# Last stage of an FFT-and-GLU backward kernel: complex product on VectorE, half spectra copied on chip, buffers reused, evacuations sorted by type

## The chip, the cores and the metric

The kernel runs on one core of a Trainium2 chip. The metric is the time of one execution on the device in microseconds (us). Five engines work side by side, each through its own queue in order: TensorE (PE, matmuls; PEld its weight loads), VectorE (DVE), ScalarE (ACT), GpSimd (POOL) and SyncE (SP, which here only issues DMAs).

## The reference

The function takes x = A_q of shape [1, 2048, 512] and returns one output and nine gradients. All tensors are bf16.

```python
xn = layernorm(x)                                   # per token, over 512 columns
k_shift = sum over t of k_pad[:, t:t+S, :] * shift_k[:, ks-1-t]   # four taps along time
kv = k_shift * v
y  = irfft(rfft(kv, 4096) * rfft(ssm_k, 4096))[:2048] + kv * ssm_D  # long convolution, per column
s  = xn * y
g  = silu( (sigmoid(xn @ w_gate) * (xn @ w_up)) @ w_down )         # GLU, width 1376
out = x + s * g
# returned: out, and the gradients for q, k, v, shift_k, ssm_k, ssm_D, w_gate, w_up, w_down
```

The gradient of the convolution is again a product of spectra, this time with a conjugate: from the gradient of y one gets the gradient of kv (with the spectrum of ssm_k) and that of ssm_k (with the spectrum of kv).

## The kernel before

**Tiling.** Time has 2048 steps; partition p holds steps 16p to 16p+15, so that an activation is a tile of 128 x (16, 512). The 512 columns are worked in four groups of 128 (`cg` = 0 to 3). The FFT of length 4096 is made of matmuls: `step1`/`step1T` multiply by 16 cosine and sine blocks, `flip`/`flipT` turn the data (by TensorE transposes in the first stage, by VectorE 32 x 32 transposes in the last), `step3`/`step3T` multiply by a small block-diagonal matrix. The way back is `inv3` and then `inv1`.

**Stages.** The first stage runs the forward long convolution (`strK`, `strV`, `strX`) beside the GLU's first half for nine of the sixteen token tiles (`f_gen`). It writes both spectra of every sixteenth part to DRAM (`KK_d`, two tiles of 128 x 1024 for each of 16 parts). The middle stage (`stepB`) runs the rest of the GLU forward and all of its backward, token tile by token tile. The last stage runs three streams: `dW()` makes the three weight gradients (35 blocks of 16 matmuls with 512 or 352 columns each, on operands that are loaded transposed from DRAM by SP), `frontC()` makes the forward transform of the gradient of y, and `backC()` multiplies it with the stored spectra, transforms it back and makes the gradients of k, v, shift_k, ssm_k and ssm_D.

**The part that is changed most, `backC`.** For every group there are four parts (`qq`), numbered n = 4 cg + qq. `step3T` leaves a spectrum in PSUM; it is copied out as `Xc` (one copy of 128 x 1024), and a second time with its two halves swapped as `Xw` (two pieces of 64 x 1024, ScalarE only). Real parts lie in partitions 0 to 63, imaginary parts in 64 to 127. For each of the two stored spectra t, two VectorE products are made, `Xc` by KK and `Xw` by KK. They are not summed on VectorE: `inv3` gets both, with one constant matrix for each, and sums them in PSUM:

```python
inv3([(PP[:, 0], RC1), (KK[:, 0], RS2)], qq - 1, B1)      # L1340
inv3([(PP[:, 1], RC1), (KK[:, 1], RS2)], qq - 1, B2, True)  # L1342
```

`inv3` makes eight matmuls of 128 columns for each of its parts, every one with weights of its own. After the four parts come `inv1` (from B1, the gradient `dkv`), the products `dks = dkv * v` and `dkv * ksh`, two small DMAs that shift the halo of `dks` by one partition, sixteen pairs of matmuls for the gradient of ssm_k (`dKT`, in a view that lies on B1's buffer), a diagonal sum on TensorE (`ps_diag`, reads `kh`), and seven VectorE instructions of 128 x 2048 for the four taps (`dk`, `term`). v is loaded and the gradients of v and k (`o3C`, `o2C`) are written for two groups at a time, 1 MB each, in rows of 512 B.

**Order of the work.** The program does not issue instructions as they are written. `Rec` records every instruction with what it reads and writes, and `order()` then plays them through a table of durations, as a list scheduler: each engine takes the recorded instruction with the lowest number among those that are ready, at most 700 numbers ahead. All engines' queues are written in that order. `run_streams` sets in which proportion the streams are recorded; `backC` is recorded to end when `dW` is at 58%. A copy out of PSUM recorded by `evac` may go to ScalarE or VectorE: ScalarE takes it unless it is late by more than 0.4 us (1.6 us where VectorE has other work soon). PSUM has, in the last stage, two slots of two banks for `step1T`, `step3T`, `inv3`, `inv1` and `dKT` together, two single banks for `dW`, and two for small work.

**Memory.** `Arena` gives out SBUF by first fit. Buffers of the last stage lie on buffers of the middle stage that were just freed.

**Layer norm.** `f_ln2` makes a small VectorE instruction for -mean * rstd (`nmr_all`) and then normalises a token tile of 128 x 512 by one ScalarE activation with that as its bias (L705, L706).

Of the kernel before, what the change touches and what calls it, by code (L numbers as in the profile page):

```python
# [20 lines left out]
D = 512  # L21
# [135 lines left out]
class Op:  # L157
    __slots__ = ("n", "alts", "deps", "succ", "wait", "ready", "dma", "tiles", "done", "fin", "eng", "soft")
# [12 lines left out]
class Rec:  # L171
# [65 lines left out]
    def evac(self, dst, src, n):  # L237
        self.add([("scalar", "copy", (dst, src), {}), ("vector", "tensor_copy", (dst, src), {})])
# [109 lines left out]
    def order(self):  # L348
# [55 lines left out]
        while ndone < len(ops):  # L404
            best = None
            for e in self.ENGS:
# [7 lines left out]
                if either and e in ("scalar", "vector"):  # L414
                    o = min(either, key=lambda o: (max(o.ready, free[e]), o.n))
                    s = (max(o.ready, free[e]), o.n, e, 1)
                    late = free["scalar"] - s[0]
# [124 lines left out]
def gen_fft_consts(nc, ar, negpi, Cf, TB):  # L542
# [65 lines left out]
    nc.vector.tensor_copy(an[:, 3], pr[:, 1])  # L608
# [16 lines left out]
def kernel_impl(ctx, tc, A_q, A_k, A_v, A_shift_k, A_ssm_k, A_ssm_D, B_x, B_w_gate, B_w_up, B_w_down,  # L625
# [32 lines left out]
    BD, RS1, RS2, RC1, BDq = (TB[:, q] for q in range(5))  # L658
# [3 lines left out]
    nmr_all = Ring(ar, [NJ], f32).ap  # L662
# [40 lines left out]
    def f_ln2(i):  # L703
        xj, st = T[i]["xq"], T[i]["st"]
        nc.vector.scalar_tensor_tensor(nmr_all[:, i:i + 1], st[:, 6:7], -1.0, rstd_all[:, i:i + 1], ALU.mult, ALU.mult)  # L705
        nc.scalar.activation(xnA[:, i, :], xj, ACT.Identity, bias=nmr_all[:, i:i + 1], scale=rstd_all[:, i:i + 1])  # L706
# [582 lines left out]
    def ld_KK(n):  # L1289
        if n < 16:  # L1290
            KK = KK_r.next()
            nc.sync.dma_start(KK, KK_d[n // 4, n % 4].rearrange("t p x -> p t x"))
            stC["KK", n] = KK

# [9 lines left out]
    def ld_bwd(cg):  # L1304
        c0, c1 = cg * GW, (cg + 1) * GW
        if cg % 2 == 0:
            stC["vg"] = vg_r.next()
            nc.sync.dma_start(stC["vg"], vC[:, :, c0:c0 + 256])
# [7 lines left out]
    def backC():  # L1316
        for cg in range(NG):
# [3 lines left out]
            for qq in range(5):  # L1321
                if qq < 4:
                    n = cg * 4 + qq
                    while ("Qf", cg) not in stC:
                        yield 0
                    Xc, Xw = Xc_r.next(), Xw_r.next()
# [3 lines left out]
                    KK = stC.pop(("KK", n))  # L1330
                    PP = P_r.next()
                    for t in range(2):
                        nc.vector.tensor_tensor(PP[:, t], Xc, KK[:, t], ALU.mult)
                        nc.vector.tensor_tensor(KK[:, t], Xw, KK[:, t], ALU.mult)
                    ys[qq] = (PP, KK)
                if qq == 2:
                    ld_bwd(cg)
                if qq > 0:
                    PP, KK = ys.pop(qq - 1)
                    inv3([(PP[:, 0], RC1), (KK[:, 0], RS2)], qq - 1, B1)  # L1340
                    yield 2048
                    inv3([(PP[:, 1], RC1), (KK[:, 1], RS2)], qq - 1, B2, True)  # L1342
                    ld_KK(cg * 4 + qq + 2)
                    yield 2048
# [3 lines left out]
            vg = stC["vg"][:, :, (cg % 2) * GW:(cg % 2 + 1) * GW]  # L1348
# [6 lines left out]
            dKT = ar.view(B1_r.blks[0][0], [128, NJ], bf16)  # L1355
# [10 lines left out]
            if cg % 2 == 1:  # L1366
                nc.sync.dma_start(o3C[:, :, c0 - GW:c1], y2A[:, :, c0 - GW:c1])
# [11 lines left out]
            if cg % 2 == 0:  # L1379
                stC["dk"] = dk_r.next()  # L1380
            dk = stC["dk"][:, :, (cg % 2) * GW:(cg % 2 + 1) * GW]
            for lag in range(4):
# [4 lines left out]
                else:  # L1387
                    term = term_r.next()
# [4 lines left out]
            if cg % 2 == 1:  # L1393
                nc.sync.dma_start(o2C[:, :, c0 - GW:c1], stC["dk"])
# [31 lines left out]
    KK_r = Ring(ar, [2, 1024], n=3)  # L1426
    Qg_r = Ring(ar, [4096])
    Ci_r = Ring(ar, [2, 16, 128], at=dg_r.blks[0][0])
# [4 lines left out]
    Xc_r, Xw_r, P_r = Ring(ar, [1024], n=2), Ring(ar, [1024], n=2), Ring(ar, [2, 1024], n=2)  # L1433
    vg_r = Ring(ar, [NJ, 2 * GW])
    ksh_r = Ring(ar, [NJ, GW])
    kh_r = Ring(ar, [NJ + 3, GW])
    term_r = Ring(ar, [NJ, GW])
    dk_r = Ring(ar, [NJ, 2 * GW])
# [9 lines left out]
    for n in range(3):  # L1448
        ld_KK(n)
    nc.sync.dma_start(Ci.rearrange("p c j n -> p (c j n)"), Ci_d[:])  # L1450
# [70 lines left out]
```

## Time and profile before

| what | value |
|---|---|
| median of the three runs | 527.73 us (527.04 to 529.77) |
| the profiled execution | 528.14 us, of which the span on the engines 526.4 us |
| PE busy over the span | 491.4 us (93%) |
| DVE busy | 403.5 us (77%) |
| ACT busy | 342.4 us (65%) |
| POOL busy | 124.1 us (24%) |
| granted TensorE clock | 0.997 |

By stage, in us (busy time of each engine within the stretch):

| stretch | length | PE | DVE | ACT | POOL | what runs |
|---|---|---|---|---|---|---|
| 0 to 27 | 27 | 14.7 | 21.2 | 20.7 | 10.5 | loads, constants |
| 27 to 150 | 123 | 113.6 | 98.1 | 120.7 | 54.0 | first stage |
| 150 to 170 | 20 | 18.4 | 15.2 | 11.8 | 5.0 | transposed weights arrive |
| 170 to 336 | 166 | 162.7 | 147.3 | 68.9 | 51.9 | middle stage |
| 336 to 363 | 27 | 26.8 | 11.4 | 8.0 | 1.5 | its end, `dW`, `frontC` of group 0 |
| 363 to 504 | 141 | 137.0 | 101.5 | 107.9 | 1.2 | `backC` with `dW` and `frontC` |
| 504 to 526.4 | 22.4 | 18.1 | 8.7 | 4.3 | 0.0 | rest of `dW`, last taps, last writes |

How to read it: an engine's busy time counts its instructions, not its waiting. Matmuls are pipelined, so PE's busy time is a little more than what its work would need at best. A row of a group list gives the engine, the operation, out<-in by the program's names, the shapes, the count, then busy time in us and the mean in ns of one, then the idle time just before and what ended it. Here nearly every tile lies in one SBUF buffer called slab, and every instruction is issued by one helper line, so groups are told apart by shape and by time.

### The profile page before, as it was taken

The page shows a single profiled execution, that of the slowest core. Times are in us where ns is not written, and L with a number is a line of the kernel's source. Part 1 is how long each engine was busy: PE and PEld are TensorE (multiplying, and loading weights), DVE is VectorE, ACT ScalarE, POOL GpSimd, SP SyncE. Part 2 cuts the span into 40 slices and gives each one's busy share as a digit, 9 for nine tenths or more (in the row PEclk, how much of TensorE's full clock was granted, in tenths as well). Part 3 has the DMA queues.
Part 4 walks back from the last instruction along what each step waited for, and adds up shares of the span by engine and source line. Part 5 has one row for each costly group of instructions (what it writes and reads, how often), then busy time and mean ns, then how long its engine had stood idle before and what let it go on. Part 6 is the DMA issues. An engine that isn't in the chain of part 4 may idle for free.

```text
span 526.4 us, 13494 instructions
## 1 busy us (share of the span) xinstructions
PE 491.4 (93%) x5373; PEld 349.4 (66%) x5429; DVE 403.5 (77%) x777; ACT 342.4 (65%) x455; POOL 124.1 (24%) x241
## 2 busy tenths in 40 slices
PE   4697899999998999999999999999999999999996
PEld 2686787898986676577775555554575665775744
DVE  7859999975759879978789999645758768883754
ACT  6899999999974345344443353335878968786621
POOL 5152533444604323424153221010000000000000
PEclk9899999999999999999999999999999999999999
DMA  8977796878999764647499936999799789999983
GB/s 261 257 223 272 227 350 200 266 238 249 215 177 256 141 169 147 200 133 169 136 215 262 211 124 201 212 291 225 185 241 240 183 248 248 244 196 247 198 228 118
DMA packets 173713, 113.19 MB, mean 215 GB/s; under 512 B 114487, under 2 KB 158161, under 8 KB 173394
## 3 DMA queue, kind: packets, MB, share of 16 engines
q1 hardware_dynamic: 162016, 78.43, 62.5%
q0 software_dynamic: 11104, 33.89, 20.9%
q8 instruction: 42, 0.69, 0.5%
q14 instruction: 21, 0.17, 0.1%
q10 hardware_dynamic: 530, 0.01, 0.1%
HBM read 37.65 MB, written 45.72 MB: 158 GB/s over the span
## 4 chain that ended last, share of the span: by engine, by line
PE 49%; DVE 22%; ACT 10%; issue 8%; DMA 5%; SPq 3%; POOL 2%; DVEq 0%; POOLq 0%; ACTq 0%
PE psum L512 49%; DVE slab L512 22%; ACT slab L512 10%; SPq L512 3%; DMA ksh_d<-slab 2%; DMA slab<-in_A_q_dram 1%; DMA slab<-in_B_w_up_dram 1%; DMA slab<-in_A_k_dram 1%; DMA Ci_d<-slab 1%; POOL slab L512 1%; POOL KK_d L512 1%; POOL hF_d L512 1%; POOL ksh_d L512 0%; POOL sF_d L512 0%; DVEq L512 0%
## 5 line engine op out<-in xcount | busy, mean ns | idle before, releaser
L512 PE MATMUL psum<-slab 128*128 128x128 bf16 (+4 forms) x5373 | 491.4, 253 | 30.8 <-ACT slab L512 14.1
L512 PEld LDWEIGHTS <-slab 128*128 128x128 bf16 (+2 forms) x5429 | 349.4, 99 | 172.4 <-issue 22.1
L512 DVE TENSOR_TENSOR slab<-slab 128x512 bf16<-128x512 bf16 (+6 forms) x472 | 268.5, 608 | 46.9 <-ACT slab L512 23.2
L512 ACT CAST slab<-psum 128x1024 bf16<-128x1024 f32 (+3 forms) x270 | 219.6, 861 | 95.5 <-PE psum L512 70.9
L512 ACT ACTIVATE slab<-psum 128x512 bf16<-128x512 f32 (+2 forms) x80 | 55.6, 695 | 47.3 <-PE psum L512 44.8
L512 ACT ACTIVATE slab<-slab 128x512 bf16<-128x512 bf16 (+2 forms) x53 | 42.1, 800 | 21.8 <-DVE slab L512 21.2
L512 ACT COPY slab<-psum 128x1024 bf16<-128x1024 bf16 (+1 forms) x49 | 46.9, 998 | 13.9 <-PE psum L512 13.9
L512 POOL DMA_DIRECT2D out_dram<-slab x32 | 17.4, 545 | 105.0 <-DVE slab L512 105.0
L512 DVE CAST slab<-psum 128x1024 bf16<-128x1024 f32 (+2 forms) x24 | 27.0, 1125 | 16.0 <-PE psum L512 15.5
L512 DVE TENSOR_TENSOR slab<-psum,slab 128x512 bf16<-128x512 f32 (+2 forms) x47 | 29.3, 625 | 10.5 <-ACT slab L512 5.7
L512 DVE SCALAR_TENSOR_TENSOR slab<-slab 128x512 bf16<-128x512 bf16 (+2 forms) x64 | 28.0, 438 | 7.9 <-POOL slab L512 5.7
L512 POOL DMA_DIRECT2D hF_d<-slab x48 | 26.0, 545 | 30.7 <-DVE slab L512 30.5
L512 POOL MEMSET slab<- 128x128 bf16 (+3 forms) x11 | 4.3, 400 | 118.0 <-PE psum L512 117.6
L512 DVE SCALAR_TENSOR_TENSOR slab<-psum,slab 128x512 bf16<-128x512 f32 x16 | 11.0, 688 | 22.4 <-PE psum L512 22.4
L512 POOL DMA_DIRECT2D KK_d<-slab x32 | 17.5, 546 | 22.2 <-ACT slab L512 19.1
L512 POOL DMA_DIRECT2D slab<-in_A_q_dram x29 | 16.2, 557 | 22.0 <-ACT slab L512 18.7
L512 DVE TENSOR_SCALAR slab<-slab 128x1 f32<-128x1 f32 (+9 forms) x54 | 16.4, 324 | 2.2 <-ACT slab L512 1.2
L512 DVE STREAM_TRANSPOSE slab<-slab 128x1024 f32<-128x1024 f32 x8 | 14.3, 1827 | 4.3 <-ACT slab L512 4.3
L512 POOL DMA_DIRECT2D slab<-hF_d x18 | 9.7, 541 | 10.6 <-PE psum L512 9.8
L512 POOL TENSOR_TENSOR slab<-slab 128x1 f32<-128x1 f32 x16 | 9.8, 612 | 9.5 <-DVE slab L512 9.3
L512 DVE BATCH_NORM_STATS2 slab<-slab 128x6 f32<-128x512 bf16 x16 | 11.0, 686 | 1.3 <-DMA slab<-in_A_q_dram 1.3
L512 POOL DMA_DIRECT2D slab<-in_grad_out_dram x16 | 8.6, 540 | 6.8 <-DMA out_dram<-slab 5.3
(20 smaller groups left out, 32.6 us busy)
## 6 DMA issues: line engine op xcount, KB each, us to landing
KK_d<-slab POOLq DMA_DIRECT2D x32, 256.0 KB, 4.2
slab<-KK_d SPq DMA_DIRECT2D x16, 512.0 KB, 4.4
slab<-in_A_v_dram SPq DMA_DIRECT2D x4, 1024.0 KB, 10.3
hF_d<-slab POOLq DMA_DIRECT2D x32, 128.0 KB, 3.8
slab<-slab SPq DMA_DIRECT2D x32, 128.0 KB, 4.7
out_dram<-slab POOLq DMA_DIRECT2D x32, 128.0 KB, 2.8
uF_d<-slab SPq DMA_DIRECT2D x32, 128.0 KB, 2.3
gF_d<-slab SPq DMA_DIRECT2D x32, 128.0 KB, 2.2
```

The source lines that it names most:

```text
L512: getattr(getattr(self.nc, eng), meth)(*[place(v) for v in a], **{x: place(v) for x, v in k.items()})
```

## The change

- **Last stage, product.** KK's one ring of three 128 x (2, 1024) tiles becomes two rings of three, `KR` and `KI`. A DMA of 256 KB loads only the real half of both spectra into partitions 0 to 63 of `KR`, another of 256 KB only the imaginary half into partitions 64 to 127 of `KI`; each is then copied into the other 64 partitions on chip by one instruction of 64 x 2048 (`both_halves`, ScalarE or VectorE, with a bias of 1.0 us toward VectorE). VectorE makes two products and their sum, `KR = Xc*KR + Xw*KI`, and `inv3` has one part with one matrix `RCS`. The constant tables change to fit (`an[:, 3]`, the name RC1).
- **Last stage, loads and buffers.** v is loaded whole, 2 MB in one DMA, into `vdk`; the gradient of k is made in place in it, and `o2C` and `o3C` are written once at the end, 2 MB each. `term` lies on `kh`, `dKT` on `ksh` instead of on B1. The pieces of `backC` are recorded with 1024 instead of 2048 columns for an `inv3`, 26624 instead of 34816 a group.
- **Evacuation by type.** In `evac`, a copy from a 2-byte PSUM tile (a transpose's result) gets a bias of 0.3 us toward VectorE in the order's choice; a copy from a 4-byte tile gets none.
- **Layer norm.** The normalisation becomes one VectorE `tensor_scalar` (subtract the mean, multiply by rstd); `nmr_all` and its small instruction go.

```diff
     def evac(self, dst, src, n):
-        self.add([("scalar", "copy", (dst, src), {}), ("vector", "tensor_copy", (dst, src), {})])
+        op = self.add([("scalar", "copy", (dst, src), {}), ("vector", "tensor_copy", (dst, src), {})])
+        op.bias = 0.3 if esize(src.ap.dtype) == 2 else -0.0
...
-                    o = min(either, key=lambda o: (max(o.ready, free[e]), o.n))
+                    sg = 1.0 if e == "scalar" else -1.0
+                    o = min(either, key=lambda o: (max(o.ready, free[e]) + sg * o.bias, o.n))
                     s = (max(o.ready, free[e]), o.n, e, 1)
-                    late = free["scalar"] - s[0]
+                    late = free["scalar"] - s[0] + o.bias
...
-        nc.vector.scalar_tensor_tensor(nmr_all[:, i:i + 1], st[:, 6:7], -1.0, rstd_all[:, i:i + 1], ALU.mult, ALU.mult)
-        nc.scalar.activation(xnA[:, i, :], xj, ACT.Identity, bias=nmr_all[:, i:i + 1], scale=rstd_all[:, i:i + 1])
+        nc.vector.tensor_scalar(xnA[:, i, :], xj, st[:, 6:7], rstd_all[:, i:i + 1], ALU.subtract, ALU.mult)
...
     def ld_KK(n):
         if n < 16:
-            KK = KK_r.next()
-            nc.sync.dma_start(KK, KK_d[n // 4, n % 4].rearrange("t p x -> p t x"))
-            stC["KK", n] = KK
+            KR = stC["KR", n] = KR_r.next()
+            nc.sync.dma_start(KR[0:64], KK_d[n // 4, n % 4].rearrange("t p x -> p t x")[0:64])
+
+    def ld_KI(n):
+        if n < 16:
+            KI = stC["KI", n] = KI_r.next()
+            nc.sync.dma_start(KI[64:128], KK_d[n // 4, n % 4].rearrange("t p x -> p t x")[64:128])
+
+    def both_halves(dst, src):
+        op = nc.add([("scalar", "copy", (dst, src), {}), ("vector", "tensor_copy", (dst, src), {})])
+        op.bias = 1.0
...
-        if cg % 2 == 0:
-            stC["vg"] = vg_r.next()
-            nc.sync.dma_start(stC["vg"], vC[:, :, c0:c0 + 256])
+        if cg == 0:
+            nc.sync.dma_start(vdk, vC)
...
+                    KR, KI = stC.pop(("KR", n)), stC.pop(("KI", n))
+                    both_halves(KR[64:128], KR[0:64])
+                    both_halves(KI[0:64], KI[64:128])
                     Xc, Xw = Xc_r.next(), Xw_r.next()
                     step3T(stC["Qf", cg], cg > 1, qq, Xc, Xw)
...
-                        nc.vector.tensor_tensor(PP[:, t], Xc, KK[:, t], ALU.mult)
-                        nc.vector.tensor_tensor(KK[:, t], Xw, KK[:, t], ALU.mult)
-                    ys[qq] = (PP, KK)
+                        nc.vector.tensor_tensor(KR[:, t], Xc, KR[:, t], ALU.mult)
+                        nc.vector.tensor_tensor(KI[:, t], Xw, KI[:, t], ALU.mult)
+                        nc.vector.tensor_tensor(KR[:, t], KR[:, t], KI[:, t], ALU.add)
+                    ys[qq] = KR
+                    ld_KI(n + 3)
...
-                    inv3([(PP[:, 0], RC1), (KK[:, 0], RS2)], qq - 1, B1)
-                    yield 2048
-                    inv3([(PP[:, 1], RC1), (KK[:, 1], RS2)], qq - 1, B2, True)
+                    inv3([(Y[:, 0], RCS)], qq - 1, B1)
+                    yield 1024
+                    inv3([(Y[:, 1], RCS)], qq - 1, B2, True)
...
-            vg = stC["vg"][:, :, (cg % 2) * GW:(cg % 2 + 1) * GW]
+            vg = vdk[:, :, c0:c1]
...
-            dKT = ar.view(B1_r.blks[0][0], [128, NJ], bf16)
+            dKT = ar.view(ksh_r.blks[0][0], [128, NJ], bf16)
...
-            if cg % 2 == 1:
-                nc.sync.dma_start(o3C[:, :, c0 - GW:c1], y2A[:, :, c0 - GW:c1])
+            if cg == NG - 1:
+                nc.sync.dma_start(o3C, y2A)
...
-            dk = stC["dk"][:, :, (cg % 2) * GW:(cg % 2 + 1) * GW]
+            dk = vg
...
-                    term = term_r.next()
+                    term = kh[:, 0:NJ, :]
...
-            if cg % 2 == 1:
-                nc.sync.dma_start(o2C[:, :, c0 - GW:c1], stC["dk"])
+            if cg == NG - 1:
+                nc.sync.dma_start(o2C, vdk)
...
-                        (gated(backC(), "back"), 4 * 34816, -0.05, 0.58)], until=lambda: "back" in flags)
+                        (gated(backC(), "back"), 4 * 26624, -0.05, 0.58)], until=lambda: "back" in flags)
```

## The prediction

> **What bounds the kernel now.** First the page's busy table and the same table cut by stage (length, then busy us and instructions of PE, PEld, DVE, ACT, POOL, then clock, DMA share, GB/s).
>
> ```profile
> PE 491.4 (93%) x5373; PEld 349.4 (66%) x5429; DVE 403.5 (77%) x777; ACT 342.4 (65%) x455; POOL 124.1 (24%) x241
> ```
>
> ```profile
> 27.00:150.00 123.00, 113.61 (x1731) 101.98 (x1746) 98.06 (x146) 120.74 (x149) 54.03 (x102) 1.00 0.86 246
> ...
> 170.00:336.00 166.00, 162.67 (x1536) 106.27 (x1550) 147.31 (x371) 68.91 (x122) 51.85 (x98) 1.00 0.68 175
> 336.00:363.00 27.00, 26.84 (x162) 14.14 (x164) 11.44 (x22) 8.03 (x12) 1.49 (x3) 1.00 1.01 267
> 363.00:504.00 141.00, 137.01 (x1456) 90.59 (x1474) 101.53 (x127) 107.88 (x119) 1.22 (x3) 1.00 0.97 224
> 504.00:526.40 22.40, 18.12 (x104) 9.91 (x103) 8.74 (x13) 4.30 (x9) 0.00 (x0) 1.00 0.52 162
> ```
>
> Two stages matter. From 27 to 150 ACT is busy 120.7 of 123 us and PE idles 9.4: copies out of PSUM set the pace. From 170 on PE is at 97 to 99%. In 363 to 504 ACT (77%) and DVE (72%) have room, but only about a quarter each.
>
> Then the group list, for prices: one PSUM copy on either engine by type, the products, the layer norm's activation, single-source VectorE work.
>
> ```profile
> L512 ACT CAST slab<-psum 128x1024 bf16<-128x1024 f32 x148 | 149.0, 1069 | 23.9 <-PE psum L512 15.0 <-DVE slab L512 5.5 <-DMA out_dram<-slab 2.3
> ...
> L512 ACT COPY slab<-psum 128x1024 bf16<-128x1024 bf16 x39 | 41.2, 1102 | 1.5 <-PE psum L512 1.5
> L512 ACT ACTIVATE slab<-slab 128x512 bf16<-128x512 bf16 x48 | 36.9, 771 | 19.3 <-DVE slab L512 18.6
> ...
> L512 DVE CAST slab<-psum 128x1024 bf16<-128x1024 f32 x20 | 24.4, 1221 | 9.7 <-PE psum L512 9.1 <-ACT slab L512 0.4
> ...
> L512 DVE TENSOR_SCALAR slab<-slab 128x1408 bf16<-128x1408 bf16 x9 | 4.7, 522 | 0.1
> ...
> L512 DVE COPY slab<-psum 128x1024 bf16<-128x1024 bf16 x5 | 3.4, 688 | 1.5 <-ACT slab L512 0.8 <-PE psum L512 0.7
> ```
>
> A transpose's result costs 0.69 us on DVE against 1.10 on ACT; an f32 tile is the other way round, 1.22 against 1.07. Two windows of the list give the price of a 128-column matmul: in the dense stretch 200 to 250, and in the last stage.
>
> ```profile
> L512 PE MATMUL psum<-slab 128*128 128x128 bf16 x371 | 22.3, 219 | 0.1
> ```
>
> ```profile
> L512 PE MATMUL psum<-slab 128*128 128x128 bf16 x768 | 51.2, 219 | 2.6 <-ACT slab L512 2.4
> ```
>
> That is 22.3/371 = 60 ns and 51.2/768 = 67 ns. Last, the timeline of DVE (start, length, group, count) and the waits of the last groups.
>
> ```profile
> 468.28 4.90 DVE L512 TENSOR_TENSOR slab<-slab 128x1024 bf16<-128x1024 bf16 x8
> 476.15 1.29 DVE L512 TENSOR_TENSOR slab<-slab 128x1024 bf16<-128x1024 bf16 x2 [2.98 <-DMA slab<-KK_d]
> ...
> 511.68 7.52 DVE L512 TENSOR_TENSOR slab<-slab 128x2048 bf16<-128x2048 bf16 x6 [6.22 <-DMA slab<-slab]
> ```
>
> ```profile
> ACT slab L512 <- DMA out_dram<-slab: 2.3, 1, 2.3
> ```
>
> A product in a row costs 4.90/8 = 0.61 us. The taps end at 519.2; `o2C` then holds the DMA engines from 520.4 to about 525.1. `dW`'s last copy ends at 522.7 and its write closes the span. So two chains end within about 1.5 us of each other: `dW` on PE, and `backC`'s tail. Taking PE work away shortens the first only; the second has to get shorter too.
>
> **First stage: evacuation by type and layer norm.** Of 42 transposed tiles of 1024 evacuated here, 37 are on ACT, 5 on DVE; DVE takes 10 f32 tiles. I take 29 of the 42 on DVE and no f32 tile there. DVE: 24 x 0.69 - 10 x 1.22 = +4.3 us. ACT: -24 x 1.10 + 10 x 1.07 = -15.7. The layer norm takes ten activations off ACT, 9.0 us by the stage's rows (mean 0.90). On DVE its new instruction lies between 0.15 (128x1 row) and 0.72 (the 128x512 `scalar_tensor_tensor`, which also reads per-partition scalars); nearest is TENSOR_SCALAR 128x1408, 0.52, scaled by length to 0.29. Less the small instruction (0.155) that is ten times 0.13 = +1.4. ACT and DVE together do 218.8 us in 123 (89% of two engines); with -19.0 that is 199.8, or 112 us at the same 89%. PE comes next: its 113.6 us at the 98% of the later stages need 115.9. So -7 us. Bounds: -9.4 (all PE idle gone) and +2 (no f32 tile leaves DVE and it is the later one). What would be late next are the weights' DMA transposes that hold up 150 to 168; they follow a spectrum of this stage, so they move with it. In the middle stage the other six normalisations cost DVE 0.8 us under a PE at 98%: nothing; 0.8 if that cover is gone.
>
> **Last stage: PE.** 32 `inv3` calls lose 8 matmuls each: 256 x 60 = 15.4 us (17.1 at 67 ns), 3.85 a group.
> The Trainium skill, "TensorE: Matmul & The Clock Gate", section Back-to-back issue gap, gives about 81 ns for a sustained 128-column pair; that would make 20.7 us. The rows here say 60 to 67, and they decide.
>
> **Last stage: DVE and ACT.** 32 sums at 0.61: +19.5 us. 32 copies of 64x2048: no row of this form. On DVE, TENSOR_SCALAR scaled to 2048 gives 0.69 (low end), the 128x2048 product 1.22 (high end); I take 0.69, since it too has one source. On ACT, from 0.58 for 512 and 1.02 for 1024 columns, 1.9. All on DVE: 22 us (to 39). Per group DVE gets 4.9 + 5.5 = 10.4 on top of its 25.4 (101.5/4), ACT has 27.0. DVE's 13 PSUM copies of the stage (13.6 us) move to ACT, which is a little quicker at them: -0.5 a group. Together 62.3, 31.1 per engine, where PE alone would allow a group in 35.25 - 3.85 = 31.4. That needs both engines at 99%. At the 89% that the first stage reaches, a group takes 35.0: -0.25 x 4 = -1.0 us. Copies for n = 0 to 2 can go before 363, where DVE idles 15.6 us of 27: 6 x 0.69 off the groups, -2.3 us at the same 89%. So the saved matmuls are mostly not seen at the end.
> POOL is busy 1.22 us of these 141, so nothing of its work is priced here.
> The Trainium skill, "GPSIMD Engine Reference", section Specifications, speaks against the change: GpSimd shares its SBUF interfaces with VectorE and contends with VectorE instructions that have two SBUF inputs, of which 32 are added. By the page some time could only be added; no row of this stage shows any.
>
> **Buffers and DMAs.** The wait of ACT above (2.3 us, at 478.6 to 480.9) is `inv3` of a group held by the write of `dKT` out of B1's buffer; `dKT` now lies on `ksh`: -2.3. What waits instead is `ksh`'s next load, and `kh`'s next load waits for the last tap, since `term` lies on it; both are SP entries, and behind them stand KK loads and `dW`'s transposed loads, so a misjudged order can stall both, 0 to 4.5 us (the two KK waits of DVE, 4.5 in total); I take 0 as SP's order is planned by due times. SP issues 16 more KK DMAs at 0.43 (6.9 us spread over the stage) and 3 fewer large ones. v comes as 2 MB (1 MB lands in 10.3 us) about 25 us before its use: hidden, 4 us if not. At the end `o2C` is 2 MB: the 1 MB now takes 3.6 us at the 289 GB/s it reached; at the 409 GB/s of the best slice near the end 2 MB take 5.1, at 289 GB/s 7.2: +1.5 to +3.6, I take +2.6.
>
> **The sum.** First stage -7.0; last stage -1.0 - 2.3 - 2.3 + 2.6 = -3.0. Together -10.0: from the profiled 528.14, which is 0.4 above the median of the runs, 518.1; from the median 517.7.
>
> **Rivals.**
> - Slower: VectorE becomes the bound of `backC`. Its four groups need 4 x 35.8 = 143 us of DVE, with the 13.6 us of PSUM copies that it makes now, in a stage of 141. If 60% of the added 41.5 us falls on the chain it is +25; with -7 and the write's +2.6 and none of the PE gain: 548 at worst, 538 where 35% does. For it: in 400.5 to 418.7 DVE is already busy without a gap, taps first. Against it: it idles 40 us in the stage, and its PSUM copies can go to ACT. It decides (over 530.4) from about 7 us, 17% of the added, beyond the PE gain.
> - `backC` is not shortened and the first stage is: 527.7 - 7 + 2.6 = 523, up to 528 with a stalled SP queue.
> - All of it is seen: -9.4 - 15.4 - 2.3 = 500.6, some 506 with the larger write and half the idle left. For it: `dW` fills PE whenever `backC` waits. Against it: the 99% above.
> - The evacuation rule changes nothing, as PE or DMA (share 0.86) holds the first stage: 527.7 - 3.0 = 524.7.
>
> **How the numbers follow.** Forecast (511 to 522) 0.39; all seen (500 to 510) 0.14; `backC` not shortened (522 to 528) 0.18; rule without effect (522 to 526) 0.10; slower (531 to 548) 0.19. A measurement of this kernel can tell about 0.5%, 2.6 us, from no change. Faster than 525.1 are the first two, half of the third and most of the fourth: 0.70; within 0.11; slower 0.19. The range leaves out 0.06 below and 0.14 above: 505 to 532; the forecast's own is 511 to 522.
>
> **What would show it.** First stage: ACT's COPY rows of bf16 go from 39 toward 15, DVE's from 5 up, PE over 96% in 27 to 143. Last stage: 512 instead of 768 128-column matmuls; DVE over 85%; `dW` used up earlier, and PE idle at the end before the last taps if the chain of `backC` sets the end. If instead the end is a `dW` copy with DVE at leisure, more of the 15 us is seen and I am too high. A copy of 64x2048 that costs 1.2 us or stands on ACT at 1.9, or DVE waits on KK_d above 4.5 us, make me too low.

## The result and the profile after

The changed kernel takes 547.31 us (542.97 to 556.26, four runs) against 527.38 us for the kernel before on the same chip: ratio 1.0345, 95% interval 1.0267 to 1.0423. It is slower. The prediction, 517.7 us with a range of 505 to 532, was wrong in sign. The profile of that first measurement was of a disturbed execution (556.26 us, which the ratio leaves out), so the lines below are from a repeat of the same kernel (e1_again below), with a span of 544.2 us.

The page's busy table, and the same table cut by stage (length, busy us and instructions of PE, PEld, DVE, ACT, POOL, then clock, DMA share, GB/s):

```profile
PE 484.1 (89%) x5122; PEld 340.4 (63%) x5173; DVE 439.3 (81%) x828; ACT 356.2 (65%) x452; POOL 124.5 (23%) x241
```

```profile
27.00:150.00 123.00, 112.61 (x1728) 102.19 (x1741) 103.52 (x150) 110.82 (x132) 51.92 (x98) 0.99 0.84 238
...
371.00:517.00 146.00, 134.55 (x1164) 81.20 (x1177) 125.66 (x167) 127.35 (x134) 1.22 (x3) 0.98 0.91 194
517.00:544.20 27.20, 12.79 (x151) 8.06 (x148) 11.99 (x16) 4.44 (x8) 0.00 (x0) 0.81 0.56 209
```

ACT lost 9.9 us of work in 27 to 150, as intended (120.7 to 110.8), and yet PE did no more matmuls there (1728 against 1731). In the last stage PE fell from 97% to 92%, and it idles 14.4 of the last 27.2 us, at a clock of 0.81.

The group list says what became of the instructions; the matmul row is of the last stage alone:

```profile
L514 ACT COPY slab<-psum 128x1024 bf16<-128x1024 bf16 x33 | 33.4, 1039 | 3.2 <-PE psum L514 3.1
...
L514 ACT COPY slab<-slab 64x2048 bf16<-64x2048 bf16 x12 | 22.8, 1897 | 2.4 <-DMA slab<-KK_d 2.2
...
L514 DVE COPY slab<-slab 64x2048 bf16<-64x2048 bf16 x20 | 13.7, 688 | 1.0 <-DMA slab<-KK_d 0.3
...
L514 DVE COPY slab<-psum 128x1024 bf16<-128x1024 bf16 x11 | 7.5, 685 | 2.5 <-PE psum L514 1.4 <-ACT slab L514 1.1
L514 DVE TENSOR_SCALAR slab<-slab 128x512 bf16<-128x512 bf16 x16 | 6.6, 410 | 3.8 <-POOL slab L514 3.5
```

```profile
L514 PE MATMUL psum<-slab 128*128 128x128 bf16 x512 | 38.3, 228 | 9.8 <-ACT slab L514 5.9 <-DVE slab L514 3.5
```

The 256 matmuls are gone, and the new copies cost what was estimated. The evacuation rule moved six tiles to DVE (5 to 11), not 24. Last, the tail on DVE and then on SP's queue (start, length, group, count, idle before and its releaser), and SP's queue in the kernel before:

```profile
516.95 3.62 DVE L514 TENSOR_TENSOR slab<-slab 128x2048 bf16<-128x2048 bf16 x3 [2.20 <-ACT slab L514]
...
529.31 7.52 DVE L514 TENSOR_TENSOR slab<-slab 128x2048 bf16<-128x2048 bf16 x6 [5.83 <-DMA slab<-slab]
```

```profile
518.20 0.60 SPq L514 DMA_DIRECT2D slab<-slab  x1
519.50 3.51 SPq L514 DMA_DIRECT2D out_dram<-slab  x3
523.06 1.10 SPq L514 DMA_DIRECT2D slab<-slab  x1
524.28 12.92 SPq L514 DMA_DIRECT2D out_dram<-slab  x6
```

```profile
504.40 4.75 SPq L512 DMA_DIRECT2D out_dram<-slab  x4
509.20 0.88 SPq L512 DMA_DIRECT2D slab<-slab  x1
```

`dks` of the last group begins at 516.95. Its taps need two small halo DMAs; the second stands on SP behind three writes, and DVE waits 5.83 us. In the kernel before it stands behind four, issued 7.1 us after `dks` began (502.10), and the taps start 2.5 us later (511.68). Here it is issued after 6.1 us, but the taps start only 6.2 us later: it lands just behind the first of the three writes, which is `o3C`. That write is now 2 MB and takes 8.6 us from its issue at 519.50 to its landing, against 6.7 us for the 1 MB before.

To see where the time went, three marks are used below, all from DVE's timeline: the end of the middle stage (its last accumulator read from PSUM), the start of `dks` of the last group, and the start of the last run of taps.

| run | end of middle stage | from there to `dks` of group 3 | to the last taps | to the end of the span |
|---|---|---|---|---|
| before | 351.5 | 150.6 | 160.2 | 174.9 |
| changed | 359.3 | 157.6 | 170.0 | 184.9 |

Of 17.8 us, 7.8 were lost before the last stage and 10.0 in it: 7.0 up to `dks`, 2.8 between `dks` and the taps, and 0.2 behind. The first column alone varies by chance: eleven profiles of kernels whose edits leave the first stage alone lie between 350.3 and 356.0. The other columns are distances within a stage.

### The profile page after: what moved, and what is told of

Its sections match the earlier page's. It is cut to its first block, busy times and chain, and to the rows that moved or that the text cites. A ratio compares the mean times of both kernels' runs of the same rounds, so it can differ in the third digit from the quotient of the medians.

```text
span 554.5 us, 13046 instructions
## 1 busy us (share of the span) xinstructions
PE 488.7 (88%) x5122; PEld 341.9 (62%) x5173; DVE 439.4 (79%) x828; ACT 356.3 (64%) x452; POOL 124.3 (22%) x241
## 4 chain that ended last, share of the span: by engine, by line
PE 53%; DVE 19%; ACT 10%; DMA 8%; issue 5%; SPq 3%; POOL 1%; DVEq 0%; ACTq 0%; POOLq 0%
PE psum L514 53%; DVE slab L514 19%; ACT slab L514 9%; DMA slab<-slab 4%; SPq L514 3%; DMA slab<-in_A_k_dram 1%; DMA slab<-in_B_w_up_dram 1%; DMA slab<-in_A_ssm_k_dram 1%; POOL slab L514 1%; DMA slab<-in_grad_out_dram 1%; POOL hF_d L514 0%; POOL KK_d L514 0%; ACT L514 0%; DVEq L514 0%; ACTq L514 0%
## 5 line engine op out<-in xcount | busy, mean ns | idle before, releaser
L514 PE MATMUL psum<-slab 128*128 128x128 bf16 (+6 forms) x5122 | 488.7, 258 | 52.2 <-DVE slab L514 19.2
L514 PEld LDWEIGHTS <-slab 128*128 128x128 bf16 (+2 forms) x5173 | 341.9, 100 | 198.6 <-issue 35.9
L514 DVE TENSOR_TENSOR slab<-slab 128x512 bf16<-128x512 bf16 (+6 forms) x504 | 290.8, 613 | 40.4 <-ACT slab L514 16.5
L514 ACT CAST slab<-psum 128x1024 bf16<-128x1024 f32 (+4 forms) x278 | 223.1, 847 | 86.0 <-PE psum L514 66.1
L514 ACT COPY slab<-psum 128x1024 bf16<-128x1024 bf16 (+1 forms) x42 | 38.5, 942 | 20.0 <-PE psum L514 19.8
L514 ACT ACTIVATE slab<-slab 128x512 bf16<-128x512 bf16 (+2 forms) x37 | 28.1, 769 | 9.8 <-DVE slab L514 9.3
L514 DVE SCALAR_TENSOR_TENSOR slab<-slab 128x512 bf16<-128x512 bf16 (+1 forms) x48 | 25.6, 533 | 2.6 <-ACT slab L514 1.4
L514 ACT COPY slab<-slab 64x2048 bf16<-64x2048 bf16 x12 | 22.8, 1897 | 3.8 <-DMA slab<-KK_d 3.6
L514 DVE CAST slab<-psum 128x1024 bf16<-128x1024 f32 (+1 forms) x16 | 17.8, 1120 | 7.4 <-PE psum L514 6.3
L514 DVE COPY slab<-slab 64x2048 bf16<-64x2048 bf16 (+1 forms) x24 | 14.3, 597 | 1.9 <-DMA slab<-KK_d 1.3
```

The costliest lines, as they stand in the source:

```text
L514: getattr(getattr(self.nc, eng), meth)(*[place(v) for v in a], **{x: place(v) for x, v in k.items()})
```

## The experiments

### Which part costs what

**e1_again** is the changed kernel once more.

> The changed kernel once more, for a profile to set beside the one of before. If the loss is steady, the three places of the first profile come back: the weights' last transposed load lands some 6 us later than before (175 against 169 us), the middle stage waits twice on a DMA transpose (some 8 us in all), and from the last layer-norm gradient to the end it takes some 9 us more (185 against 175.5). If a part of this was chance of one execution, that part is gone here and the span is 541 to 546 us.

544.9 us, 1.0272 (1.0189 to 1.0354).

**e2_last** has the last stage's change without the evacuation rule and with the old layer norm:

```diff
-        op.bias = 0.3 if esize(src.ap.dtype) == 2 else -0.0
+        op.bias = 0.0
...
-        nc.vector.tensor_scalar(xnA[:, i, :], xj, st[:, 6:7], rstd_all[:, i:i + 1], ALU.subtract, ALU.mult)
+        nc.vector.scalar_tensor_tensor(nmr_all[:, i:i + 1], st[:, 6:7], -1.0, rstd_all[:, i:i + 1], ALU.mult, ALU.mult)
+        nc.scalar.activation(xnA[:, i, :], xj, ACT.Identity, bias=nmr_all[:, i:i + 1], scale=rstd_all[:, i:i + 1])
```

> The last stage's part of the change alone: evacuation without a bias by type, layer norm on ScalarE as before. Theory A, VectorE is the bound of the last stage and its chain got longer: most of the loss is here, 536 to 543 us, with the first stage as before (last transposed weight at 168 to 170 us). Theory B, the loss comes from the first stage and the middle (order of the queues after bias and layer norm moved): 524 to 531 us.

541.37 us, 1.0246 (1.0167 to 1.0325). Its middle stage ends at 354.4, and its last stage takes the same 184.9 us as the whole change's.

**e3_front** is the other half: evacuation rule and new layer norm, with the last stage of before.

> Evacuation by type and layer norm on VectorE alone, last stage as before. Theory A: 519 to 527 us, as my prediction had it (-7 for the first stage). Theory B: 534 to 541 us, with the transposed weights late by some 6 us and waits on DMA transposes in the middle stage.

537.36 us, 1.0130 (1.0043 to 1.0217); the middle stage ends at 360.7. **e5_bias** has the evacuation rule alone, **e6_xn** the layer norm on VectorE alone.

> Evacuation by type alone. Together with the layer norm it cost some 8 us. If the bias is the cause (transposed tiles queue behind the 128x2048 products on VectorE): 533 to 540 us, first KK_d store at 35 to 38 us instead of 30.8. If the layer norm is: 525 to 531 us.

> Layer norm on VectorE alone. If it is the cause of the loss in the first stage (normalised tiles and constants queue up on VectorE in the first 27 us): 533 to 540 us, with 112 instead of 159 PE instructions in the first 27 us. If the bias is: 525 to 531 us. If neither alone but both together: both 525 to 531.

540.28 us, 1.0189 (1.0115 to 1.0263), and 544.87 us, 1.0233 (1.0102 to 1.0363). In both, nearly all of the loss lies before the last stage: the middle stage ends at 364.2 and 364.4. Each part alone costs as much as both together or more. Costs that simply add up cannot do that; something else is hit or missed by each order.

### Order alone

Three kernels keep the instructions of the kernel before (the planner moves one to three copies between ACT and DVE) and only alter constants of the planner: how many instruction numbers ahead it may take (e4_nudge), the time that it allows from a PSUM result to its reader (e12_psl), and the shares of the last stage's streams (e16_bpace).

```diff
-LOOK = 700
+LOOK = 690
...
-PSL = 0.25
+PSL = 0.30
...
-    live = run_streams([(dw[0], dw[1] - dw[4], 0.0, 1.0), (frontC(), 4 * 4096, -0.05, 0.44),
-                        (gated(backC(), "back"), 4 * 34816, -0.05, 0.58)], until=lambda: "back" in flags)
+    live = run_streams([(dw[0], dw[1] - dw[4], 0.0, 1.0), (frontC(), 4 * 4096, -0.05, 0.36),
+                        (gated(backC(), "back"), 4 * 34816, -0.05, 0.48)], until=lambda: "back" in flags)
```

> The kernel before with the scheduler's look-ahead at 690 numbers instead of 700: the same work and the same engines, only another order. It says how much the time moves by a reordering that means nothing. If the written order is robust: 525 to 531 us. If any reordering costs several us, because the kernel's order fits this chip by choice: 531 to 540 us, and then no part of the change under that size can be read from its time alone.

528.66 us, 0.9988 (0.9954 to 1.0023). Not every new order costs time. This one leaves SP's queue almost as it was: of its 310 entries in the trace, told apart by operation and names, 308 stand in the same order as before, against 293 (e12) and 289 (e16) in the next two kernels.

> The kernel before with one constant of the planner altered (PSL, the time it allows from a PSUM result to its reader, 0.30 for 0.25): the same instructions in another order on all engines from the start. Theory 'fitted order': the order of the kernel before was chosen with its instructions, and any other order costs some 5 to 15 us, because what collides is found by trial: 533 to 543. Theory 'work': the loss in the first stage came from the instructions that moved, not from the order as such: 526 to 531.

542.88 us, 1.0259 (1.0186 to 1.0331): 14 us with no work added. In its profile the middle stage ends 8.1 us later than before and the last stage takes 182.0 us (174.9).

> The kernel before with the shares of the last stage's streams altered as in the earlier run (frontC 0.36, backC 0.48): the same instructions, the first and middle stage in the same order, another order in the last stage alone. It says what order alone is worth in the last stage: from the end of the middle stage to the end of the span 174.9 us in the kernel before. Theory 'fitted order': 179 to 185, 532 to 538 us, so that a large part of the change's 10 us could be order. Theory 'work': 173 to 177, 526 to 531, so that the 10 us are the added copies and sums and the write at the end.

538.98 us, 1.0183 (1.0119 to 1.0246); the last stage takes 181.7 us. So the kernel before is fitted to its order, and an order is as much part of a change as its instructions. The next runs ask what the bad orders run into.

### The first stage: what a small DMA stands behind

In the first stage every spectrum of K is copied once more with its halves swapped (`Ks`), by two DMAs of 128 KB on SP. The evacuation rule alone (e5), on SP and on DVE:

```profile
138.96 4.70 SPq L514 DMA_TRANSPOSE slab<-in_B_w_down_dram  x1
143.71 1.38 SPq L514 DMA_DIRECT2D slab<-slab  x1
145.13 14.38 SPq L514 DMA_TRANSPOSE slab<-in_B_w_down_dram  x3
```

```profile
157.61 0.69 DVE L514 TENSOR_TENSOR slab<-slab 128x1024 bf16<-128x1024 bf16 x1 [7.72 <-DMA slab<-slab]
```

The last of the swapped halves is issued at 143.71, between the weights' transposed loads, and its reader starts 13.9 us later. DVE waits 7.72 us for it and PE in turn 6.4 us for DVE; the clock between 150 and 165 falls to 0.70. Just ahead of this, PE waits 3.3 us for ACT, which waits for a store to `KK_d`. The two waits on PE, and an estimated 3.4 us for 6.7 us of matmuls at half the clock (149.22 to 151.94 and 158.36 to 162.36), make 13.1 us; the middle stage ends 12.7 us later than before. In the kernel before, the entries stand in much the same order, but the DMA is issued at 137.06, and DVE's product uses it at 144.64 without a wait:

```profile
137.06 0.59 SPq L512 DMA_DIRECT2D slab<-slab  x1
```

**e11_swapbias** takes the DMAs of the last group away:

```diff
-                nc.sync.dma_start(Ks[0:64], KF[64:128])
-                nc.sync.dma_start(Ks[64:128], KF[0:64])
+                if cg == 3:
+                    nc.vector.tensor_copy(Ks[0:64], KF[64:128])
+                    nc.vector.tensor_copy(Ks[64:128], KF[0:64])
+                else:
+                    nc.sync.dma_start(Ks[0:64], KF[64:128])
+                    nc.sync.dma_start(Ks[64:128], KF[0:64])
```

> The evacuation rule alone, but in the last group of the first stage the two swapped halves of the spectrum of K are copied by VectorE (eight copies of 64x1024) in place of two DMAs each on SP. Theory 'transposes': with the rule alone the last of these DMAs stands behind three of the weights' transposed loads on SP, VectorE waits 7.7 us for it, PE 6.4 us for VectorE and the clock falls; that is where the 11 to 13 us went. Without these DMAs: 528 to 534 us against 540.3. Theory 'balance': the rule gives VectorE and ScalarE a worse share of the copies throughout the stage: 538 to 543.

530.58 us, 1.0009 (0.9973 to 1.0046). The whole loss is gone, and both waits with it: PE runs from 129.8 to 175.2 without a gap. With the sum above, this says that the loss came from late DMAs in this stretch (e11 is another order too, so that the run alone would not say it); and the rule itself, once it collides with nothing, is worth nothing.

Why these DMAs are late is not separated: they stand behind transposed loads on SP, and the DMA engines are busy throughout (share 1.20 in 135 to 150 in e5). e11 takes away both the place on SP and 1 MB of copies. DMAs of another queue are late here too. Of the stores to `KK_d`, which POOL issues, one lands 11.8 us after its issue at 145.40 in the kernel before, and one 13.5 us after its issue at 144.40 in e6. In e6 a long wait hangs on it: ACT waits 8.44 us for it, DVE 8.7 us for ACT and PE 8.1 us for DVE. No run undid this one.

The order-only kernel e12 has the same wait as e5 in its waits of 60 to 180 (total, times, longest), which was not undone there:

```profile
DVE slab L512 <- DMA slab<-slab: 6.3, 1, 6.3
```

**e13_afterswap** is the same cure for the whole change.

> The whole change, with the two swapped halves of the last group's spectra of K copied by VectorE (eight copies of 64x1024) in place of the DMAs on SP, as in the run that took the evacuation rule alone back to the time of the kernel before. Theory 'transposes': the first stage's loss of the whole change (the middle stage ends at 359.3 us of the span against 351.5) comes from DMAs that meet the weights' transposed loads: it ends at 351 to 354, and the time is 537 to 541 us, the last stage's 10 us staying. Rival: in the whole change no wait of 6 us on these halves stands in the profile, what is late is the start-up and the taps on VectorE, and the weights then come 3.4 us late all the same: it ends at 357 to 361, the time is 542 to 547.

547.11 us, 1.0357 (1.0295 to 1.0420). It does not help; the middle stage ends at 356.8, 2.5 us earlier than in the repeat of the change, which is within chance. The whole change's order had no long wait on these halves. The repeat's first stage is late otherwise: PE does 113 matmuls in 15 to 30 at a clock of 0.77 (168 at 0.89 before), 157 in 60 to 75, where DVE is busy 14.74 of 15 us (220 before), and PE waits 3.4 us for the last load of `w_up` (1.4 before). e13 has the first two of these as well (114 and 160 matmuls), not the third. Which of these sets the 7.8 us was not settled by a run.

### The last stage: the chain, the tail and SP's queue

**e7_nocopy** leaves out the 32 copies (the other halves stay as set to zero once), **e8_nosum** the 32 sums (the product with `KI` is not used); both on e2.

```diff
-                    both_halves(KR[64:128], KR[0:64])
-                    both_halves(KI[0:64], KI[64:128])
...
-                        nc.vector.tensor_tensor(KR[:, t], KR[:, t], KI[:, t], ALU.add)
```

> The last stage's part alone, without the 32 copies of 64x2048: the other halves of KR and KI are set to zero once, so the products use zeros or old values there. It takes 22.8 us off ScalarE and 13.8 us off VectorE in the last stage. Theory A, VectorE and ScalarE bound the chain of backC and the copies tip it: 527 to 533 us, against 541 with them. Theory C, the loss is the larger writes at the end and the order of the DMAs: 537 to 542 us.

> The last stage's part alone, without the 32 sums of 128x1024 on VectorE (the product with KI is made and not used). It takes 19.6 us off VectorE and nothing off ScalarE. If VectorE's load itself is what counts, as much is won as without the copies or more: 526 to 533 us. If ScalarE's 1.9 us copies in the way of PSUM copies are: 536 to 541 us.

538.41 us, 1.0135 (1.0055 to 1.0214), and 540.09 us, 1.0175 (1.0102 to 1.0248). That looks as if neither mattered much. The marks say otherwise: `dks` of group 3 comes 148.4 and 151.0 us behind the middle stage, 9.2 and 6.6 earlier than in e2. The time is lost again behind it, in the chain of waits of e7 (start, length, what was waited for) and in the waits of e8's last stage:

```profile
508.10 8.66 DMA slab<-uF_d
```

```profile
DVE slab L514 <- PE psum L514: 20.1, 6, 13.9
```

In e7 a transposed load of `dW` comes late and PE stands still for 5.2 us; in e8 DVE waits 13.9 us for a small result that PE makes only after `dW`'s blocks ahead of it in its queue.

**e9_pace** records `dW` later among `backC`'s work in e2 (the shares 0.36 and 0.48 above); **e10_pairs** writes `o2C` and `o3C` per pair of groups again.

```diff
-            if cg == NG - 1:
-                nc.sync.dma_start(o2C, vdk)
+            if cg % 2 == 1:
+                nc.sync.dma_start(o2C[:, :, c0 - GW:c1], vdk[:, :, c0 - GW:c1])
```

> The last stage's change alone, with the shares of the streams altered: frontC 0.36 and backC 0.48 in place of 0.44 and 0.58, so that dW's matmuls are put later among those of backC. Nothing else differs. Theory 'filler': in the last stage's change alone PE does 155 matmuls of 512 columns before the products dks of group 0 (107 in the kernel before) and is then idle in 14.4 of the last 27.3 us (4.4 of 24.3 before); the order was set for a backC that used more of PE. With dW later the groups end earlier and PE's idle time at the end is filled: 533 to 538 us against 541.4. Theory 'chain': the sequence of VectorE and ScalarE work of backC sets the end wherever dW stands: 540 to 543. Rival: dW, now later, becomes the end itself: over 543.

> The last stage's change alone, with the gradients of v and k written per pair of groups (1 MB each) as in the kernel before, not as one 2 MB write behind the last tap. The prediction's step: the larger write costs 1.5 to 3.6 us, 2.6 taken, so 537.8 to 539.9 against 541.4, and the span ends about 4 us behind the last tap instead of 7.4. Rival: the write of the first pair only takes the DMA engines from the loads of KK earlier in the stage, and nothing is gained: 540.5 to 543.

540.25 us, 1.0213 (1.0145 to 1.0281), and 542.91 us, 1.0224 (1.0151 to 1.0297). Neither differs from e2 by more than the intervals. In e10 the stretch from `dks` of group 3 to the end is 24.3 us, as in the kernel before (27.3 in e2), so the smaller writes do what was hoped for at the end. But `dks` comes 164.1 us behind the middle stage (157.6 in e2), and nothing is left of it; what made it late was not tested.

**e14_lasthalo** issues the two halo DMAs of e2 from POOL, which is idle in this stage; **e17_bhalo** does the same to the kernel before.

```diff
-            nc.sync.dma_start(dks[0:112, NJ:NJ + 3, :], dks[1:113, 0:3, :])
-            nc.sync.dma_start(dks[112:127, NJ:NJ + 3, :], dks[113:128, 0:3, :])
+            nc.gpsimd.dma_start(dks[0:112, NJ:NJ + 3, :], dks[1:113, 0:3, :])
+            nc.gpsimd.dma_start(dks[112:127, NJ:NJ + 3, :], dks[113:128, 0:3, :])
```

> The last stage's change alone, with the two halo DMAs of dks of each group issued from POOL, which has nothing to do there, in place of SP, where three writes stand between them and the taps wait 5.8 us. Theory: the end is the chain of the last taps and the 2 MB write behind them; the wait falls to 2 to 4 us, and the time by 2 to 4 us, to 537.5 to 539.5 against 541.4. Rival: the halo takes as long from POOL, or dW's write ends last: 540.5 to 543.

531.75 us, 1.0059 (1.0022 to 1.0096): of the last stage's 2.46%, 1.87 points are gone with two small DMAs per group, much more than was expected. Its timeline, POOL and DVE:

```profile
505.68 1.06 POOL L514 DMA_DIRECT2D slab<-slab  x2 [9.80 <-DVE slab L514]
```

```profile
504.15 3.62 DVE L514 TENSOR_TENSOR slab<-slab 128x2048 bf16<-128x2048 bf16 x3 [4.27 <-ACT slab L514]
...
511.17 7.52 DVE L514 TENSOR_TENSOR slab<-slab 128x2048 bf16<-128x2048 bf16 x6
```

The taps follow `dks` after 7.0 us (12.4 in e2) without a wait. It helps in every group: in e2 the second halo DMA of group 2 is issued at 489.55, 16.8 us after the start of its `dks` at 472.80, and taps pile up before later sums; here each pair goes out at once. From the end of the middle stage it is 152.2 us to `dks` of group 3 (157.6) and 177.9 to the end (184.9).

> The kernel before with the halo DMAs of dks issued from POOL in place of SP, as was done to the last stage's change. It gives the kernel that the last stage's change has to be compared with once both are rid of that wait. Theory 'queue': before has the wait too, 6.2 us behind four writes, but dW's last matmuls and write end 1.3 us behind its taps' write, so it gains 1 to 4 us, 525 to 528.5 against 529.4, and the change's last stage, at 531.7 with the same cure, is 3 to 7 us dearer by its copies, sums and write. Rival: it gains as much as the change did, 9 us (519 to 522), and the change's own work costs the full 10. Rival: the wait is covered by dW and nothing is gained: 528.5 to 531.

527.09 us, 0.9979 (0.9942 to 1.0017): no measurable gain, though the chain is far shorter. Its timeline on DVE, and ACT's copy of `dW`'s last block:

```profile
492.06 3.62 DVE L512 TENSOR_TENSOR slab<-slab 128x2048 bf16<-128x2048 bf16 x3 [5.25 <-ACT slab L512]
498.36 7.52 DVE L512 TENSOR_TENSOR slab<-slab 128x2048 bf16<-128x2048 bf16 x6 [1.67 <-DMA slab<-slab]
```

```profile
522.18 0.45 ACT L512 CAST slab<-psum 128x352 bf16<-128x352 f32 x1 [1.94 <-PE psum L512]
```

`dks` of group 3 begins 140.0 us behind the middle stage, the taps at 146.3, and yet the end stands where it stood, because `dW` on PE ends at 522.2 as before. In the kernel before, PE is the bound of this stage and the chain of `backC` had slack. This gives the like-for-like figure: with the cure on both sides the chain to `dks` is 12.2 us longer with the change (152.2 against 140.0), and the end comes 4.7 us later (177.9 against 173.2), 0.8% by the times. `dW`'s last copy comes 168.8 us behind the middle stage against 170.2: of 256 matmuls saved, 1.4 us.

These 4.7 us are not the longer chain itself. In e14 the last taps end at 518.69, ahead of `dW`'s last copy (520.81). What ends last is `o2C`: it stands on SP behind the write of `dW`'s last block, is issued at 521.74, 3.0 us after the taps, and its 2 MB land 7.0 us later. Its entry, and its line in the list of DMA issues (KB, us to landing):

```profile
521.74 0.36 SPq L514 DMA_DIRECT2D out_dram<-slab  x1
```

```profile
out_dram<-slab SPq DMA_DIRECT2D x1, 2048.0 KB, 7.0
```

In e17 the 1 MB write goes out earlier, and `dW`'s last write, issued at 522.66, ends the span at 525.2. No run moved `o2C` in e14.

**e18_bpacehalo** puts the cure on the order-only kernel e16, whose tail was (DVE, then SP):

```profile
519.85 7.52 DVE L512 TENSOR_TENSOR slab<-slab 128x2048 bf16<-128x2048 bf16 x6 [17.80 <-DMA slab<-slab]
```

```profile
509.90 0.61 SPq L512 DMA_DIRECT2D slab<-slab  x1
510.61 6.93 SPq L512 DMA_DIRECT2D out_dram<-slab  x7
517.59 0.88 SPq L512 DMA_DIRECT2D slab<-slab  x1
```

> The kernel before with the altered shares of the last stage (frontC 0.36, backC 0.48) and the halo DMAs on POOL. With the shares alone the products dks of the last group began 141.8 us behind the end of the middle stage (150.6 before), and then the taps waited 17.8 us for the halo, which stood on SP behind seven writes; that cost 9.4 us. Theory 'queue': without that wait the taps begin some 7 us behind dks, dW fills the rest, and the time is 521 to 528. Theory 'order': the loss lies in the order of the engines' work, and the time is 534 to 540.

532.48 us, 1.0069 (1.0035 to 1.0103). Six of e16's nine us come back, so most of its loss was the same wait. What ends last now is `dW`, which these shares put later: its last write is issued 174.6 us behind the middle stage, against 170.6 in e17.

**e15_poolcopy** has POOL make the 32 copies of e2.

```diff
-        op = nc.add([("scalar", "copy", (dst, src), {}), ("vector", "tensor_copy", (dst, src), {})])
-        op.bias = 1.0
+        nc.gpsimd.tensor_copy(dst, src)
```

> The last stage's change alone, with the 32 copies of 64x2048 made by POOL, which is busy 1.8 us of the stage, in place of VectorE (20 of them, 0.69 us each) and ScalarE (12, 1.90 each). Theory 'chain': copies on VectorE and ScalarE lengthen the chain from the end of the middle stage to the products dks of the last group, 157.6 us against 150.6 before; without them that was 148.4, and it should be 148 to 152 here; the time is 533 to 538 if the end behind dks stays at 27.3 us, up to 541 if the taps then wait for dW's matmuls ahead of them on PE, as they did without copies. Rival: a copy on POOL takes longer than the 2.1 us that a product's wait can hide, or slows VectorE, and the chain is 155 or longer: 540 to 550.

567.10 us, 1.0725 (1.0658 to 1.0793). A copy takes 2.16 us on POOL, but VectorE pays. Group lists of the last stage, e2 and then e15:

```profile
L514 DVE TENSOR_TENSOR slab<-slab 128x1024 bf16<-128x1024 bf16 x96 | 62.7, 688 | 9.5 <-ACT slab L514 7.8
L514 DVE TENSOR_TENSOR slab<-slab 128x2048 bf16<-128x2048 bf16 x36 | 43.7, 1224 | 11.8 <-DMA slab<-slab 5.8 <-ACT slab L514 5.1
```

```profile
L514 DVE TENSOR_TENSOR slab<-slab 128x1024 bf16<-128x1024 bf16 x96 | 83.0, 905 | 5.9 <-ACT slab L514 3.1 <-issue 1.1 <-POOL slab L514 0.6
L514 DVE TENSOR_TENSOR slab<-slab 128x2048 bf16<-128x2048 bf16 x36 | 54.3, 1519 | 7.9 <-DMA slab<-slab 5.3 <-ACT slab L514 1.6
```

The same 132 products take 30.9 us longer (83.0 + 54.3 against 62.7 + 43.7). The Trainium skill, "GPSIMD Engine Reference", section Specifications, says that GpSimd shares its SBUF interfaces with VectorE and contends with VectorE instructions that have two SBUF inputs; these rows agree, with 32% and 24% on instructions of just that kind. VectorE's instructions with one input from SBUF keep their time in the same lists (STREAM_TRANSPOSE 1822 and 1827 ns).

No run beats the kernel before by more than its interval; e17_bhalo (0.9979) is level with it.

## Why the prediction was wrong

- **"First stage -7.0": failed, and in sign.** The step took the engine with the fullest row, ACT at 120.7 of 123, for the bound and let the stage shrink with ACT's and DVE's sum at 89%. ACT did fall by 9.9 us, and the stage got longer. Inside it the sizes were off too: 6 tiles moved, not 24, and a normalisation costs 0.41 us on DVE, not 0.29. The term that was missing is what a new order does to the DMAs of the stage: with the rule alone, late DMAs cost some 10 us, and e11 shows the rule without them at 1.0009. That is the price of the rival "the evacuation rule changes nothing". For the whole change the cause of the 7.8 us stays open.
- **"The weights' DMA transposes ... move with the stage": wrong where it was tested.** In e5 they stand in the way of the stage: the spectra that they were to follow need DMAs in the same queue.
- **"PE -15.4 mostly not seen": right.** The matmuls went, and 1.4 us of them show at `dW`'s end.
- **Prices of the copies: right** (0.69 and 1.90 us, as 0.69 and 1.9). **"Six copies before 363, -2.3": half.** Three of the six stand ahead of the corresponding point, two of them on ACT at 1.90.
- **"At 89% a group takes 35.0, -1.0": failed.** The sum of work per engine said that the chain keeps pace. Copies and sums lengthen it by 12.2 us like for like, 29% of the 41.5 added. The rival "VectorE becomes the bound of `backC`" has this mechanism, with a threshold of 17%, but its price is not confirmed: with the halo cured the taps no longer end last, and the 4.7 us at the end are `o2C`'s place on SP and its size. (In the stretch quoted for that rival, 400.5 to 418.7, eight products come ahead of the taps.)
- **"0 to 4.5; I take 0 as SP's order is planned by due times": the largest miss in the last stage.** The danger was seen, looked for in the KK loads (whose wait on DVE went from 4.5 to 0.3, with 2.2 on ACT), and set to nothing. In fact it lay in the halo DMAs, whose 6.22 us of waiting stood in the lines shown of before. Out of the queue they are worth 9.9 us (1.87%) to the changed last stage and 1.1 us, within the interval, to the kernel before.
- **"dKT: -2.3": the wait of ACT is gone, the time is not.** e17 shortens the same chain by 10.6 us and gains nothing that can be measured, so in the kernel before it did not set the end.
- **"+2.6 for the 2 MB write": near in size, but mostly at another place.** The stretch from `dks` to the end grew by 3.0 us, and with 1 MB writes (e10) it is 24.3 again. Behind the taps it is 14.9 us against 14.7; there 2 MB take 6.3 us to land and 1 MB 5.4 (e2, e10). The rest is the halo, which lands behind `o3C`.
- **The slower side** was given 0.19 at 531 to 548 us, and the total fell there, but by luck: its working had the first stage at -7 and the last at +17 to +27; measured are +8 and +10.

## What to carry to other kernels

Follow a queue that several streams share, entry by entry, before any engine's busy sum: a DMA of a few us whose reader stands on the chain, behind transposed loads or writes of another stream, cost 10 us twice here. Move such a DMA to a queue that is idle (the halo), or make the copy on an engine with room (VectorE in e11; on POOL in e15 it cost more than it saved). Look first whether DMAs of other queues land late in the same stretch: then another queue may not help. Measure the change against a base with the same cure. And when a planner writes the order, run one or two controls with the same instructions in another order first: here they cost up to 2.6%, more than most of the parts under test.

## What the hardware showed that was not expected

- A transposed load of `w_down` can hold SP's queue for several us, and by very different amounts: three in a row took 12.1 us before, 14.4 in e5 and 17.6 in e6, four took 9.15 in e11, each time with the DMA engines' share above 1.1. What sets it was not tested.
- POOL's copies slowed VectorE's two-input products by 24 to 32%.
- Gaps on PE cost twice. After gaps of 2.87 and 2.25 us between its matmuls (423 to 426 and 464 to 466), with shorter ones beside them, the last stage of e2 has a granted clock of 0.89 in 420 to 435 and in 465 to 480; the kernel before has 1.00 throughout that stage. The Trainium skill, "TensorE: Matmul & The Clock Gate", section Part 1: The HAM clock gate, says that the clock halves after an idle window of about 3.4 us and needs as long a busy one to return; the rows here agree in the length (0.89 over 15 us is a half clock for an estimated 3.3 us), while the gaps ahead of it are shorter than that window; for the gaps the rows decide.
